# Feed-forward matmuls as pairs on the 128x64 halves of the array: a state-space convolution with a gated feed-forward

## The chip, the cores and the metric

The kernel runs on one core of one Trainium2 chip. Its time is the device time of one execution, in microseconds (us). The engines are named as the profile names them: PE is TensorE (PEld its weight loads), DVE VectorE, ACT ScalarE, POOL GpSimd, and SP the engine that issues most of the DMAs.

## What is computed

Everything is bfloat16, with one batch, 2048 positions and 512 channels. Cut to what matters:

```python
xn = layernorm(x)                                  # x = A_q, 2048 x 512
k_shift = sum(shift(k, t) * shift_k[:, t] for t in range(4))
kv = k_shift * v
y = irfft(rfft(kv, 4096) * rfft(ssm_k, 4096))[:2048] + kv * ssm_D
s = xn * y                                         # branch A: a long convolution
g = silu((gelu(xn @ w_gate) * (xn @ w_up)) @ w_down)   # branch B: 512 -> 1792 -> 512
out = x + s * g
```

The change concerns the three products of branch B: gate and up (512 to 1792) and down (1792 to 512).

## The kernel before

**Branch B** works in four quarters `q` of 512 positions, and in 14 units `m` of 128 hidden channels. `unit(q, m)` multiplies the 128 columns `m` of `Wg` and of `Wu` (four matmuls each, over the 512 inputs in blocks of 128) with the transposed quarter `xnT`, 512 positions wide, each product into a PSUM bank of its own. ScalarE takes the Gelu of the gate bank into `GE` (L1194), and VectorE multiplies it with the up bank into `HT` (L1203; for some units a copy `U_` of the up bank is multiplied instead, L1200). In the first quarter units 0 and 1 are cut to pieces of 128 positions (`N_HALF`), so that they can begin before the whole quarter is transposed. `down(q)` then sums, for each 128 positions of a quarter, 14 matmuls of `HT` with `Wd`, 512 columns wide, into one bank; the last 128 positions of the last quarter are cut into 384 and 128 columns.

**Branch A** is a transform of length 4096 in two stages. Its first stage uses the array as two halves of 64 rows (64x128 tiles; L959 for the filter, L950 for `kv`), its second stage and the first stage of the inverse use 16 tiles of 32x32 (L1028, in bursts of 16 or 32 matmuls), and the last stage of the inverse uses two halves of 64 columns (128x64 tiles, L1278). Between these stages the data go through DRAM (`ZH`, `ZK`, `ZI`). The filter `Hn` is first transposed on the whole array (L916).

**Three ways of using the array** matter here. A whole matmul (L641, by the helper `mm`) uses 128 rows and 128 columns. A pair on halves is two matmuls with `tile_position` (0, 0) and (0, 64): each has all 128 rows and 64 of the output rows (64 of the array's columns), both stream the same right-hand side, and together they fill the same 128 partitions of one bank. The downs of the last quarter were such pairs already (L1224), all but the last piece of 128 columns, since they lie among the pairs of L1278.

**Order.** The order of all engines' instructions is a list written out by hand (`SEQ`); `S.run()` walks it, gives out buffers (at most four single banks for branch B) and estimates times, from which the choice of buffers follows. A task's `mode` tells that estimate how the array is split. `trk.op` issues an instruction with the waits that its buffers need.

Of the kernel before, what the change touches and what calls it, by code (L numbers as in the profile page):

```python
# [17 lines left out]
KD = DM // 128  # L18
MF = FF // 128
NQ = 4  # L20
# [35 lines left out]
SMALL = 1.15 * 262144  # L56
T_FWD = 219.0
N_HALF = 2
UNITS = [(0, 6), (0, 8), (0, 10), (0, 12), (1, 0), (1, 2), (1, 4), (1, 6), (1, 8), (1, 10), (1, 12)]


# [352 lines left out]
def build_kernel(nc, A_q, A_k, A_v, A_shift_k, A_ssm_k, A_ssm_D, B_w_gate, B_w_up, B_w_down, out):  # L414
    with ExitStack() as es0:
# [18 lines left out]
        Wd = new("Wd", [128, MF, DM], BF16)  # L434
# [22 lines left out]
        xnT = new("xnT", [128, 2, 4, KD, 128], BF16)  # L457
# [6 lines left out]
        HT = new("HT", [128, 2, MF, 512], BF16)  # L464
# [51 lines left out]
        trk = Trk(nc, block)  # L516
# [9 lines left out]
        def bank(b):  # L526
            return PSALL[:, 512 * b.slot:512 * (b.slot + 1)]
# [4 lines left out]
        def R_bank(b):  # L532
            return [R_ps[b.slot // 2][b.slot % 2]]
# [106 lines left out]
        def mm(h, o, l, r, st, sp):  # L640
            return h.matmul(o, lhsT=l, rhs=r, start=st, stop=sp)  # L641


        B = Buf
        bX = [[B(f"X{q}_{t}") for t in range(4)] for q in range(NQ)]
# [137 lines left out]
        R_Wc = {}  # L783
# [381 lines left out]
        def unit(q, m):  # L1165
            ci = (m + 2) // 4
            pg, pu = B(f"psg{q}_{m}", pF), B(f"psu{q}_{m}", pF)
            g = B(f"ge{q}_{m}", pGE)

            def half(p, W, nm, j0=0, j1=4):  # L1170
                def f(e):
                    for kd in range(KD):
                        trk.op("PE", lambda h, kd=kd: mm(h, bank(p)[:, 128 * j0:128 * j1], W[:, kd, 128 * m:128 * (m + 1)], xnT[:, q % 2, j0:j1, kd, :], kd == 0, kd == KD - 1),
                               r=[R_Wc[nm, ci], *R_xnT[q % 2][j0:j1]], w=R_bank(p), accum=True)
                return f
            if q == 0 and m < N_HALF:

                for i in range(2):
                    c = slice(256 * i, 256 * i + 256)
                    p2 = [B(f"psg{q}_{m}_{i}", pF), B(f"psu{q}_{m}_{i}", pF)]  # L1180
                    g2 = B(f"ge{q}_{m}_{i}", pGE)
                    for p, W, nm in ((p2[0], Wg, "g"), (p2[1], Wu, "u")):
                        for j in (2 * i, 2 * i + 1):
                            gu_tasks[q].append(S.add([("PE", pe(4, 128))], half(p, W, nm, j, j + 1), r=[bW[nm][ci], bxnT[q][j]], w=[p], lat=150.0))
                    op([("ACT", act(256))], lambda e, h, p=p2[0], g=g2, c=c: h.activation(GE[:, g.slot, c], bank(p)[:, c], ACTF.Gelu_apprx_tanh), r=[p2[0]], w=[g2],
                       rr=lambda p=p2[0]: R_bank(p), ww=lambda g=g2: [R_GE[g.slot]], after=sin_tasks)
                    op([("DVE", dve(256, 1))], lambda e, h, p=p2[1], g=g2, c=c: h.tensor_tensor(HT[:, 0, m, c], bank(p)[:, c], GE[:, g.slot, c], ALU.mult), r=[p2[1], g2], w=[bHT[q][m]],
                       rr=lambda p=p2[1], g=g2: R_bank(p) + [R_GE[g.slot]], ww=[R_HT[0][m]])
                return
            tg = S.add([("PE", pe(4))], half(pg, Wg, "g"), r=[bW["g"][ci]] + bxnT[q], w=[pg], lat=150.0)  # L1190
            tu = S.add([("PE", pe(4))], half(pu, Wu, "u"), r=[bW["u"][ci]] + bxnT[q], w=[pu], lat=150.0, after=[tg])
            gu_tasks[q] += [tg, tu]
            af = sin_tasks if q == 0 else []
            op([("ACT", act(512))], lambda e, h: h.activation(GE[:, g.slot, :], bank(pg), ACTF.Gelu_apprx_tanh), r=[pg], w=[g],  # L1194
               rr=lambda: R_bank(pg), ww=lambda: [R_GE[g.slot]], after=af)
            af = (down_tasks[q - 2] if q >= 2 else []) + (s1_tasks["H"] if q == 1 else [])
            if (q, m) in UNITS:
                ub = B(f"ub{q}_{m}", pU)
                op(EV(512), lambda e, h: copy(e, h, U_[:, ub.slot, :], bank(pu)), r=[pu], w=[ub], rr=lambda: R_bank(pu), ww=lambda: [R_U[ub.slot]])
                op([("DVE", dve(512, 2))], lambda e, h: h.tensor_tensor(HT[:, q % 2, m, :], U_[:, ub.slot, :], GE[:, g.slot, :], ALU.mult), r=[ub, g], w=[bHT[q][m]],  # L1200
                   rr=lambda: [R_U[ub.slot], R_GE[g.slot]], ww=[R_HT[q % 2][m]], after=af)
                return
            op([("DVE", dve(512, 1))], lambda e, h: h.tensor_tensor(HT[:, q % 2, m, :], bank(pu), GE[:, g.slot, :], ALU.mult), r=[pu, g], w=[bHT[q][m]],  # L1203
               rr=lambda: R_bank(pu) + [R_GE[g.slot]], ww=[R_HT[q % 2][m]], after=af)

        def down(q):
            for jt in range(4):
                t = 4 * q + jt
                cols = [(0, DM)] if t < NT - 1 else [(0, 384), (384, DM)]
                for c0, c1 in cols:  # L1210
                    p = B(f"psd{q}_{jt}_{c0}", pF)

                    def pc(p=p, c0=c0, c1=c1):
                        return bank(p)[:, c0:c1]

                    for m0, m1 in ((0, 4), (4, 9), (9, 14)):
                        paired = q == NQ - 1 and c1 - c0 > 128

                        def f(e, p=p, jt=jt, m0=m0, m1=m1, pc=pc, c0=c0, c1=c1, paired=paired):
                            for m in range(m0, m1):  # L1220
                                if paired:
                                    for i in range(2):
                                        c = slice(64 * i, 64 * i + 64)
                                        trk.op("PE", lambda h, m=m, i=i, c=c: h.matmul(pc()[c, :], lhsT=HT[:, q % 2, m, 128 * jt + 64 * i:128 * jt + 64 * i + 64], rhs=Wd[:, m, c0:c1], start=m == 0, stop=m == MF - 1, tile_position=(0, 64 * i)),  # L1224
                                               r=[R_HT[q % 2][m], R_Wd[m // 7]], w=R_bank(p), accum=True)
                                    continue
                                trk.op("PE", lambda h, m=m: mm(h, pc(), HT[:, q % 2, m, 128 * jt:128 * (jt + 1)], Wd[:, m, c0:c1], m == 0, m == MF - 1),
                                       r=[R_HT[q % 2][m], R_Wd[m // 7]], w=R_bank(p), accum=True)
                        down_tasks[q].append(S.add([("PE", pe(m1 - m0, c1 - c0))], f, r=(bHT[q] if jt else bHT[q][m0:m1]) + bWd[m0 // 7:(m1 + 6) // 7],
                                                   w=[p], lat=150.0, mode=3 if paired else 0))  # L1230
                    n = c1 - c0
                    g, rg = G[:, t, c0:c1], [R_G[t] if n == DM else R_Gh[c0 > 0]]
                    bt = B(f"tanh{q}_{jt}")
                    if q < NQ - 1:
                        op([("ACT", act(n))], lambda e, h, g=g, pc=pc: h.activation(g, pc(), ACTF.Tanh, scale=0.5), r=[p], w=[bt],  # L1235
                           rr=lambda p=p: R_bank(p), ww=rg, after=h_tr_tasks + (h2_tasks if q >= 2 else []))
                        op([("DVE", dve(512, 1))], lambda e, h, g=g, pc=pc: h.scalar_tensor_tensor(out=g, in0=g, scalar=1.0, in1=pc(), op0=ALU.add, op1=ALU.mult),  # L1237
                           r=[p, bt], w=[bG[t // 2]], rr=lambda p=p, rg=rg: R_bank(p) + rg, ww=rg)
                        continue

                    u, x = XN[:, t, c0:c1], X[:, t, c0:c1]
                    b2 = B(f"o{t}_{c0}")
                    op([("ACT", act(n))], lambda e, h, g=g, pc=pc: h.activation(g, pc(), ACTF.Silu), r=[p], w=[bt],
                       rr=lambda p=p: R_bank(p), ww=rg, after=zh_tasks + h2_tasks)
                    op([("DVE", dve(n, 2))], lambda e, h, g=g, u=u: h.tensor_tensor(g, g, u, ALU.mult), r=[bt, bS[t // 2]], w=[b2], rr=rg + [R_XN[t]], ww=rg)
                    op([("DVE", dve(n, 2))], lambda e, h, g=g, x=x: h.tensor_tensor(g, g, x, ALU.add), r=[b2], w=[b2], rr=rg + [R_X[t]], ww=rg)
                    R_o, d_o = trk.free_res(f"outl{t}_{c0}"), dsem(f"d_outl{t}_{c0}")
                    d_out.append(d_o)
                    S.add([("SP", ISSUE)], lambda e, t=t, c0=c0, c1=c1, g=g, rg=rg, R_o=R_o, d_o=d_o: dma(e, out_dr[:, t, c0:c1], g, d_o, rg, [R_o]),
                          r=[b2], w=[B(f"outl{t}")], nbytes=256 * n)  # L1250
# [114 lines left out]
```

## Time and profile before

| | |
|---|---|
| median of 3 runs | 189.29 us (189.12 to 190.32) |
| the profiled execution | 189.28 us, of which 187.5 us are the span from its first to its last instruction |
| TensorE busy | 182.2 us, 1451 recorded matmuls, 1459 weight loads |
| VectorE, ScalarE, GpSimd busy | 164.8, 140.0, 12.9 us |
| DMA | 48.37 MB, mean 258 GB/s |

The page gives each engine's busy time as a share of the span. Matmuls overlap in the array, so the duration of one (about 0.38 us for 512 columns) is longer than its share of the stream; what one costs in a row of many is seen from the starts, or from the pieces of the chain of waits, which run from end to end.

### The profile page before, as it was taken

Reading aid. Unit: us, or ns where it says so; the run is one execution under the profiler, and the core shown is the slowest. Engines: PE = TensorE matmul, PEld = TensorE weight load, DVE = VectorE, ACT = ScalarE, POOL = GpSimd, SP = SyncE. Lnnn points to the kernel's source line nnn. Section 1 sums busy time; section 2 is a strip of 40 time slices with the busy share of each in tenths; the row PEclk is TensorE's granted clock in tenths of the full one; section 3 lists DMA queues with packets and bytes.
Section 4 is the critical chain, followed back from the end, with each engine's and each line's share of the span. In section 5 each row is a group of like instructions: output and inputs, shape, how many; then the busy total and the mean of one; then the engine's idle time right before and its main releaser. Section 6 shows DMA issues by size and latency. Waiting matters only on the chain.

```text
span 187.5 us, 3669 instructions
## 1 busy us (share of the span) xinstructions
PE 182.2 (97%) x1451; PEld 80.5 (43%) x1459; DVE 164.8 (88%) x249; ACT 140.0 (75%) x193; POOL 12.9 (7%) x26
## 2 busy tenths in 40 slices
PE   8899999999999999999999999999999999999993
PEld 3585443444334344334434433434333334445552
DVE  6897999999999999969459999998899994468995
ACT  3766697898698979888878779888887863144961
POOL 4502304100000000020200000000000000000000
PEclk9999999999999999999999999999999999999999
DMA  5999999999938695777999991869327056699226
GB/s 156 352 404 299 373 374 377 394 404 245 326 87 330 225 337 212 241 260 241 290 268 261 352 343 65 298 229 334 108 111 277 0 168 217 228 325 385 83 101 235
DMA packets 38502, 48.37 MB, mean 258 GB/s; under 512 B 9427, under 2 KB 28119, under 8 KB 38486
## 3 DMA queue, kind: packets, MB, share of 16 engines
q1 hardware_dynamic: 31958, 39.76, 64.1%
q10 hardware_dynamic: 6528, 8.39, 12.6%
q8 instruction: 11, 0.18, 0.5%
q14 instruction: 5, 0.04, 0.1%
HBM read 27.39 MB, written 14.68 MB: 224 GB/s over the span
## 4 chain that ended last, share of the span: by engine, by line
PE 91%; DVE 3%; DMA 2%; ACT 1%; issue 1%; POOL 0%
PE psall L641 71%; PE psall L1224 6%; PE psall L1028 6%; PE psall L950 2%; PE psall L959 2%; PE psall L916 2%; PE psall L1278 2%; DMA X<-in_A_q_dram 2%; ACT BO L632 1%; DVE stats L849 1%; DVE KAC L1005 1%; PE psall L892 0%; DVE XN L871 0%; DVE XN L965 0%; DVE HT L1203 0%
## 5 line engine op out<-in xcount | busy, mean ns | idle before, releaser
L641 PE MATMUL psall<-xnT,Wu 128*128 128x512 bf16 (+1 forms) x248 | 56.5, 359 | 0.0
L641 PE MATMUL psall<-xnT,Wg 128*128 128x512 bf16 (+1 forms) x248 | 55.8, 359 | 0.0
L1194 ACT ACTIVATE GE<-psall 128x512 bf16<-128x512 f32 x54 | 31.9, 606 | 13.6 <-PE psall L641 11.1
L641 PE MATMUL psall<-Wd,HT 128*128 128x512 bf16 (+1 forms) x174 | 38.3, 367 | 0.8 <-issue 0.6
L1203 DVE TENSOR_TENSOR HT<-psall,GE 128x512 bf16<-128x512 f32 x43 | 29.3, 682 | 7.8 <-PE psall L641 7.5
L641 PEld LDWEIGHTS psall<-xnT,Wu 128*128 128x128 bf16 x248 | 22.5, 98 | 26.1 <-issue 2.3
L641 PEld LDWEIGHTS psall<-xnT,Wg 128*128 128x128 bf16 x248 | 21.8, 98 | 26.0 <-issue 3.2
L632 ACT ACTIVATE BO<-psall 128x1024 bf16<-128x1024 f32 x20 | 19.9, 1022 | 9.4 <-PE psall L1278 4.8
L641 PEld LDWEIGHTS psall<-Wd,HT 128*128 128x128 bf16 x182 | 16.3, 98 | 21.2 <-issue 3.9
L1131 DVE TENSOR_TENSOR HSW<-KB,HSW 128x2048 bf16<-128x2048 bf16 x16 | 19.3, 1218 | 1.9 <-ACT KB L632 1.9
L632 ACT ACTIVATE HSW<-psall 128x1024 bf16<-128x1024 f32 x15 | 15.2, 1024 | 2.4 <-PE psall L1028 2.1
L632 ACT ACTIVATE KB<-psall 128x1024 bf16<-128x1024 f32 x15 | 14.6, 1026 | 0.8 <-PE psall L1028 0.8
L1011 DVE TENSOR_TENSOR KAC<-KAC,KTM 128x2048 bf16<-128x2048 bf16 x12 | 14.6, 1217 | 0.0
L1009 DVE TENSOR_TENSOR KTM<-KK,SKB 128x2048 bf16<-128x2048 bf16 x12 | 14.6, 1215 | 0.0
L632 ACT ACTIVATE AST<-psall 128x1024 bf16<-128x1024 f32 x12 | 12.1, 1032 | 0.9 <-PE psall L950 0.8
L1224 PE MATMUL psall<-Wd,HT 128*64 128x512 bf16 (+1 forms) x112 | 12.5, 366 | 0.0
L862 POOL TENSOR_TENSOR mv<-mv,NHALF 128x1 f32<-128x1 f32 (+1 forms) x7 | 7.3, 1049 | 68.6 <-DVE mv L850 48.0
L1235 ACT ACTIVATE G<-psall 128x512 bf16<-128x512 f32 x12 | 7.1, 597 | 6.3 <-PE psall L641 6.3
L849 DVE BATCH_NORM_STATS2 stats<-X 128x6 f32<-128x512 bf16 x16 | 10.5, 675 | 0.5 <-DMA X<-in_A_q_dram 0.5
L632 ACT ACTIVATE XN<-psall 128x1024 bf16<-128x1024 f32 x9 | 9.2, 1028 | 1.1 <-PE psall L959 1.0
L1237 DVE SCALAR_TENSOR_TENSOR G<-G,psall 128x512 bf16<-128x512 bf16 x12 | 7.9, 682 | 2.3 <-ACT G L1235 2.3
L1131 DVE TENSOR_TENSOR KB<-KB,HSW 128x2048 bf16<-128x2048 bf16 x8 | 9.7, 1219 | 0.1
(91 smaller groups left out, 178.3 us busy)
## 6 DMA issues: line engine op xcount, KB each, us to landing
BH<-ZH SPq DMA_DIRECT2D x8, 512.0 KB, 5.0
HSW<-HSW SPq DMA_DIRECT2D x16, 256.0 KB, 3.7
BK<-ZK SPq DMA_DIRECT2D x8, 512.0 KB, 5.9
ZI<-BO ACTq DMA_DIRECT2D x16, 256.0 KB, 2.8
BI<-ZI SPq DMA_DIRECT2D x8, 512.0 KB, 8.5
ZK<-AST SPq DMA_DIRECT2D x6, 512.0 KB, 2.9
ZH<-XN ACTq DMA_DIRECT2D x5, 512.0 KB, 4.3
Hn<-in_A_ssm_k_dram SPq DMA_DIRECT2D x4, 512.0 KB, 8.0
```

The costliest lines, as they stand in the source:

```text
L632: return h.activation(o, i, ACTF.Copy, scale=scale)
L641: return h.matmul(o, lhsT=l, rhs=r, start=st, stop=sp)
L849: t_stats[t] = op([("DVE", 670.0)], lambda e, h, t=t: h.bn_stats(stats[:, t, :], X[:, t, :]), r=[bX[q][t % 4]], w=[bst[t]], rr=[R_X[t]], w ...
L862: t_pw = op([("POOL", 2500.0 if q else 600.0)], lambda e, hd, ts=ts, n=n: hd.tensor_tensor(mv[:, ts, 3:4], mv[:, ts, 2:3], NHALF[:, 0:n, : ...
L1009: op([("DVE", dur)], lambda e, h, j=j, m=m: h.tensor_tensor(KTM[:, m.slot, :, :], kk(j), sk(j), ALU.mult), r=need + [bSKB[j], a], w=[m], r ...
L1011: op([("DVE", dur)], lambda e, h, m=m: h.tensor_tensor(KAC[:, a.slot, :, :], KAC[:, a.slot, :, :], KTM[:, m.slot, :, :], ALU.add), r=[m], ...
L1028: trk.op("PE", lambda h: h.matmul(ps(s, i)[b, :], lhsT=wt(col)[a, :], rhs=data(col)[a, :], start=n < 16, stop=n >= len(todo) - 16, tile_po ...
L1131: return hd.tensor_tensor(pair(KB, *(2 * DM * z for z in slots())) if to else x, k, x, ALU.mult)
L1194: op([("ACT", act(512))], lambda e, h: h.activation(GE[:, g.slot, :], bank(pg), ACTF.Gelu_apprx_tanh), r=[pg], w=[g], rr=lambda: R_bank(pg ...
L1203: op([("DVE", dve(512, 1))], lambda e, h: h.tensor_tensor(HT[:, q % 2, m, :], bank(pu), GE[:, g.slot, :], ALU.mult), r=[pu, g], w=[bHT[q][m]],
L1224: trk.op("PE", lambda h, m=m, i=i, c=c: h.matmul(pc()[c, :], lhsT=HT[:, q % 2, m, 128 * jt + 64 * i:128 * jt + 64 * i + 64], rhs=Wd[:, m, ...
L1237: op([("DVE", dve(512, 1))], lambda e, h, g=g, pc=pc: h.scalar_tensor_tensor(out=g, in0=g, scalar=1.0, in1=pc(), op0=ALU.add, op1=ALU.mult ...
```

## The change

Gate and up matmuls are issued as pairs on 128x64 halves in all units but 0 to 4 of the first quarter (`N_PLAIN`), and down matmuls as pairs in all quarters, except for the last piece of 128 columns. The left operand of each half is 64 of the 128 columns of the block, the right operand is the same for both. Whole matmuls stay for units 0 to 4 of the first quarter, the transposes, the warm-up and the last 128 columns. The order of the instructions on each engine and the modes that the estimate sees stay as they are: each whole matmul has two in its place.

```diff
+N_PLAIN = 5
...
+        def columns(o, l, r, st, sp, rr, ww):
+            for i in range(2):
+                c = slice(64 * i, 64 * i + 64)
+                trk.op("PE", lambda h, c=c, i=i: h.matmul(o[c, :], lhsT=l[:, c], rhs=r, start=st, stop=sp, tile_position=(0, 64 * i)), r=rr, w=ww, accum=True)
...
+            paired = q > 0 or m >= N_PLAIN
+
             def half(p, W, nm, j0=0, j1=4):
                 def f(e):
                     for kd in range(KD):
+                        if paired:
+                            columns(bank(p)[:, 128 * j0:128 * j1], W[:, kd, 128 * m:128 * (m + 1)], xnT[:, q % 2, j0:j1, kd, :], kd == 0, kd == KD - 1, [R_Wc[nm, ci], *R_xnT[q % 2][j0:j1]], R_bank(p))
+                            continue
...
-                        paired = q == NQ - 1 and c1 - c0 > 128
+                        paired = c1 - c0 > 128
...
+                                args = HT[:, q % 2, m, 128 * jt:128 * (jt + 1)], Wd[:, m, c0:c1], m == 0, m == MF - 1
+                                rw = [R_HT[q % 2][m], R_Wd[m // 7]], R_bank(p)
                                 if paired:
...
+                                    columns(pc(), *args, *rw)
+                                else:
+                                    trk.op("PE", lambda h, args=args: mm(h, pc(), *args), r=rw[0], w=rw[1], accum=True)
...
-                                                   w=[p], lat=150.0, mode=3 if paired else 0))
+                                                   w=[p], lat=150.0, mode=3 if paired and q == NQ - 1 else 0))
```

More of the change, by code (lines that the diff above doesn't have):

```diff
@@ L1216, in down @@
                     for m0, m1 in ((0, 4), (4, 9), (9, 14)):
-                        paired = q == NQ - 1 and c1 - c0 > 128
+                        paired = c1 - c0 > 128
                         def f(e, p=p, jt=jt, m0=m0, m1=m1, pc=pc, c0=c0, c1=c1, paired=paired):
                             for m in range(m0, m1):
+                                args = HT[:, q % 2, m, 128 * jt:128 * (jt + 1)], Wd[:, m, c0:c1], m == 0, m == MF - 1
+                                rw = [R_HT[q % 2][m], R_Wd[m // 7]], R_bank(p)
                                 if paired:
[L1222 to L1228, printed above, removed]
+                                    columns(pc(), *args, *rw)
+                                else:
+                                    trk.op("PE", lambda h, args=args: mm(h, pc(), *args), r=rw[0], w=rw[1], accum=True)
                         down_tasks[q].append(S.add([("PE", pe(m1 - m0, c1 - c0))], f, r=(bHT[q] if jt else bHT[q][m0:m1]) + bWd[m0 // 7:(m1 + 6) // 7],
-                                                   w=[p], lat=150.0, mode=3 if paired else 0))
+                                                   w=[p], lat=150.0, mode=3 if paired and q == NQ - 1 else 0))
                     n = c1 - c0
```

## The prediction

> **What bounds the kernel now.** First the page: the engines' shares, the granted clock, and the chain that ended last.
>
> ```profile
> PE 182.2 (97%) x1451; PEld 80.5 (43%) x1459; DVE 164.8 (88%) x249; ACT 140.0 (75%) x193; POOL 12.9 (7%) x26
> ...
> PEclk9999999999999999999999999999999999999999
> ...
> PE 91%; DVE 3%; DMA 2%; ACT 1%; issue 1%; POOL 0%
> ```
>
> TensorE is busy 97% of the span, it holds 91% of the chain, and its clock is full in all forty slices. Next, what TensorE waited for, in the list of waits filtered to it, and under it a row of the view of the tile `psall` with the whole-array down products:
>
> ```profile
> PE psall L641 <- PEq L1350: 0.8, 1, 0.8
> PE psall L641 <- issue: 0.6, 4, 0.2
> PE psall L892 <- DVE XN L871: 0.5, 1, 0.5
> PE psall L959 <- DVE HT L1203: 0.3, 1, 0.3
> ...
> L641 PE MATMUL psall<-Wd,HT x174: 219/379/390, 39.0 to 184.4; 128*128 128x512 bf16 x160, 128*128 128x128 bf16 x14
> ```
>
> These are four waits, 2.2 us in all. From about 24 us on nothing but TensorE's own stream sets the end, so the change is worth what it does to that stream. (The "issue" gaps I read as missing matmul records: the down products have 174 where the program has 168 + 14 = 182.)
>
> The chain in order of time gives that stream in pieces, each timed from the end of the piece before it to its own end: start, duration, line and number of matmuls. The last row, from the groups by line and form, is the pairs' weight loads (busy us, mean ns of one).
>
> ```profile
> 63.49 4.42 PE psall L641 x20
> ...
> 76.45 1.83 PE psall L641 x8
> ...
> 100.64 4.42 PE psall L641 x20
> 105.06 0.37 PE psall L1028 x16
> 105.43 2.69 PE psall L641 x12
> 108.12 0.58 PE psall L1028 x32
> 108.70 1.83 PE psall L641 x8
> ...
> 168.79 0.55 PE psall L1278 x4
> 169.35 1.94 PE psall L1224 x18
> ...
> 174.09 0.43 PE psall L1278 x4
> ...
> L1224 PEld LDWEIGHTS psall<-Wd,HT 128*64 128x64 bf16 x112 | 6.3, 110 | 5.2
> ```
>
> L641 pieces are whole-array matmuls, L1028 the bursts on 32x32 tiles, L1224 and L1278 the pairs on 128x64 halves that exist already. Twelve more whole matmuls (20 against 8) cost 4.42 - 1.83 = 2.59 us, so one costs 0.216. What is left of a piece, 1.83 - 8 x 0.216 = 0.10 us, is the price of entering whole-array mode, and it is the same behind 32x32 tiles (100.64, 108.70) and behind the 64x128 matmuls of L950 (63.49, 76.45).
>
> **The change: the stream itself.** 432 whole gate and up matmuls of 512 columns exist (12 undivided units of four for gate and four for up in the first quarter, 14 in each other quarter). Units 2, 3 and 4 of the first quarter keep 24 of them, so 408 become pairs, and with them the 3 x 4 x 14 = 168 down matmuls of the first three quarters. 576 matmuls become 576 pairs, 1152 matmuls of half the output rows with the same 512 columns streamed. A pair's price is in the trace: 18 matmuls of L1224, nine pairs, took 1.94 us, 0.216 a pair. That is the whole matmul's price to the last digit. Steady streaming therefore changes by 576 x 0 = 0. What hides the doubled weight loads is that they run under the matmul before: a load of a half takes 0.110 us and both of a pair run side by side (6.3 us busy for 112), beneath 0.216 of streaming. If that cover failed, 576 x 0.11 = 63 us would stand open; the 1.94 shows no part of it.
>
> [...]
>
> **The change: entering and leaving.** In the order of the changed kernel's TensorE instructions a stretch of pairs is entered 36 times at a place where a stretch of whole matmuls was entered before: 24 times from 32x32 tiles, 12 times from 64x128 matmuls. Each has an exit as before. Beside them, two switches are new early (a later unit's gate and up come there as pairs, the Hn transposes and the last of units 2 to 4 behind them whole), one is new where a transpose of Hn is followed by pairs at about 25 us, and the one at 168.7 us, where whole matmuls gave way to L1278, goes.
>
> What entering pair mode costs, the trace shows once, at 168.79: 0.55 us for two pairs that otherwise take 0.43 (174.09), so 0.12, against 0.10 for whole matmuls. The tile view shows the difference more finely (shortest, median and longest ns of one):
>
> ```profile
> L641 PE MATMUL psall<-xnT,Wg x248: 219/379/390, 7.5 to 166.7; 128*128 128x512 bf16 x108, 128*128 128x128 bf16 x16
> ...
> L1278 PE MATMUL psall<-BI,G x32: 379/379/403, 168.7 to 180.6; 128*64 128x512 bf16 x32
> ```
>
> The first matmul after a switch waits for its weights: 390 - 379 = 11 ns on the whole array, 403 - 379 = 24 on halves. I take 13 ns for each of the 36 entries: 36 x 0.013 = 0.47 us.
>
> [...]
>
> The switch itself, without the weights, in the timeline (each window opened so that the last matmul or pair before a switch stands alone):
>
> ```profile
> 118.69 0.38 PE L641 MATMUL psall<-xnT,Wu 128*128 128x512 bf16 x1
> 119.00 0.43 PE L1028 MATMUL psall<-BH,TF 32*32 32x512 bf16 x16
> 119.37 0.39 PE L641 MATMUL psall<-xnT,Wg 128*128 128x512 bf16 x1
> ...
> 168.41 0.38 PE L641 MATMUL psall<-xnT,Wu 128*128 128x512 bf16 x1
> 168.72 0.62 PE L1278 MATMUL psall<-BI,G 128*64 128x512 bf16 x4
> ...
> 183.38 0.33 PE L1224 MATMUL psall<-Wd,HT 128*64 128x384 bf16 x2
> 183.64 0.95 PE L641 MATMUL psall<-Wd,HT 128*128 128x128 bf16 x14
> ```
>
> From whole to tiles 0.31 us start to start, from whole to pairs 0.31, against 0.216 without a switch: 0.095 each. From pairs of 384 columns to whole 0.26, where 384 columns stream in 0.75 x 0.216 = 0.16: 0.10. So all kinds cost alike, whether the columns alone are re-split or both rows and columns. The 72 switches that matter (pairs to and from tiles, pairs to and from 64x128) are not in the trace. Their change is bounded below by a drain that vanishes, -0.1 each or -7 us; above, by a switch that waits until the modelled end of a matmul, 0.38 instead of 0.31 us, +0.07 each or +5. I take zero, since four kinds lie within 10 ns.
>
> The odd switches: the one that goes saves 0.12 at 168.7, the one at 25 us costs 0.12, in sum nothing. The two early ones cost 0.12 + 0.10 = 0.22 us, ahead of this wait:
>
> ```profile
> 22.02 1.21 DVE L1005 TENSOR_TENSOR KAC<-KK,SKB 128x2048 bf16<-128x2048 bf16 x1
> 23.16 0.67 DVE L1203 TENSOR_TENSOR HT<-psall,GE 128x512 bf16<-128x512 f32 x1
> ...
> 20.05 1.03 PE L641 MATMUL psall<-xnT,Wu 128*128 128x512 bf16 x4
> ...
> 23.88 0.39 PE L959 MATMUL psall<-HTr,F 64*128 64x512 bf16 x2 [0.31 <-DVE HT L1203]
> ```
>
> TensorE stands idle 0.31 us there, for an HT product that VectorE does late because KAC runs first; its up input, by the order the group that starts at 20.05, had ended at 21.08, 2 us earlier. 0.22 fits under 0.31; without that cover it is +0.22.
>
> No DMA, wait or buffer moves: the order on every engine is the same, and consumers of a pair wait for its second half. ScalarE and VectorE keep their instructions.
>
> The sum against the profiled run, 189.28 us (187.5 of span and 1.8 around it; the median is 189.29): 0 + 0.47 + 0 = 189.75, say 189.8.
>
> **The rivals.** *Cheaper switches (faster).* If a change between two column-split modes drains less than one to or from the whole array, each of the 72 gains up to 0.1 us: half of it gives 189.8 - 3.6 = 186.2, all of it 182.6. It decides beyond 1% from (1.9 + 0.5) / 72 = 33 ns a switch. For it: none of these 72 is in the trace. Against it: whole to pairs re-splits columns alone and still pays 0.095.
>
> *Instruction issue (slower).* A pair needs four instructions where a whole matmul needs two. The tightest long stretch:
>
> ```profile
> 109.00:155.60 46.60, 46.31 (x541) 18.31 (x542) 45.04 (x49) 38.77 (x50) 0.00 (x0) 1.00 0.56 191
> ...
> 7.63 1.16 PE psall L641 x20
> ```
>
> 1083 instructions in 46.6 us, 43 ns each. The bursts in it are 9 of 16 and 7 of 32 tiles, 368 matmuls; the other 173 double, so 1429 must be issued, 33 ns each. Small early matmuls were fed at 1.16 / 40 = 29 ns an instruction, but over 20 matmuls only, which a queue may have held ready. If the sustained rate lies over 33 ns, TensorE starves around the bursts: at 36 ns the stretch takes 51.4 us, +4.8, so 194.6; it passes 1% from about 34. Against it: the 1.94 of L1224 is 54 ns an instruction without strain, and matmul time alone explains the 43.
>
> **How the numbers follow.** A measurement of this kernel can't tell under about 1% (1.9 us) from no change. The forecast gets 0.72; its own spread is the early 0.22 and some ns a switch, 189.0 to 190.8. Cheaper switches get 0.18, of which 0.13 beyond 1%; issue gets 0.10, of which 0.09 beyond. So faster 0.13, same 0.72 + 0.05 + 0.01 = 0.78, slower 0.09. The range leaves out the large outcomes of both rivals: 187.4 (33 ns a switch gained) to 191.2 (1% up, or 20 ns lost a switch).
>
> **What would show it.** Right: pieces of pairs in the chain at 0.216 a pair plus 0.12 where whole ones had 0.10; bursts still 0.36 to 0.37 and 0.58; TensorE gaps as before. Wrong: the first start behind a burst of 16 other than 0.37 us after the burst's own (119.00 to 119.37), an exit from pairs unlike 0.31, or new TensorE gaps put down to issue between 109 and 156 us.

## The result and the profile after

The changed kernel takes 190.16 us (median of 22 runs, beside 189.47 for 22 runs of the kernel before): a ratio of 1.0044, 95% interval 1.0031 to 1.0056, so 0.83 us more (0.59 to 1.06). The ratio is worked out from all of these runs; the two medians alone lie 0.69 us apart. The profiled execution took 190.05 us with a span of 188.2.

The page's clock and the other engines' shares stand as before, and TensorE holds 96% of the chain that ended last, where it held 91%. What grew is TensorE's count of instructions:

```profile
PE 184.2 (98%) x2035; PEld 89.6 (48%) x2035; DVE 165.2 (88%) x249; ACT 140.4 (75%) x193; POOL 12.9 (7%) x26
...
PEclk9999999999999999999999999999999999999999
...
q8 instruction: 16, 0.26, 0.5%
...
PE 96%; DVE 2%; ACT 1%; issue 0%
```

The row `q8 instruction` is from the list of DMA queues: the number of packets and the MB in which TensorE's own program is fetched, and the share of the 16 DMA engines' time that they took. Before, the same row was

```profile
q8 instruction: 11, 0.18, 0.5%
```

That this row is TensorE's is read from its growth: the only other such row, `q14 instruction`, has 5 packets and 0.04 MB in both, and the other engines' counts stand.

The chain in order of time (start, duration, line, matmuls), the same places as before; L647 are the pairs, so 24 and 16 matmuls stand where 12 and 8 stood, and the burst lines are now L956 and L1034:

```profile
76.90 1.85 PE psall L647 x16
...
101.21 4.44 PE psall L647 x40
...
106.01 2.71 PE psall L647 x24
108.72 0.58 PE psall L1034 x32
109.31 1.85 PE psall L647 x16
...
169.64 0.43 PE psall L1287 x4
170.07 1.94 PE psall L647 x18
```

Each piece is 0.02 longer, whatever its length: 1.83 became 1.85 and 4.42 became 4.44. So twelve pairs more still cost 4.44 - 1.85 = 2.59 us, 0.216 each, and the bursts still 0.58. The 0.55 of the inverse's first two pairs at 168.79 is 0.43, as everything around it is now in pairs.

The same in the starts of two bursts far apart, from the timelines of before (L1028) and after (L1034):

```profile
81.45 0.43 PE L1028 MATMUL psall<-BH,TF 32*32 32x512 bf16 x16
...
154.87 0.65 PE L1028 MATMUL psall<-HSW,MI 32*32 32x512 bf16 x32
```
```profile
81.93 0.43 PE L1034 MATMUL psall<-BH,TF 32*32 32x512 bf16 x16
...
155.70 0.65 PE L1034 MATMUL psall<-HSW,MI 32*32 32x512 bf16 x32
```

The second kernel is 0.48 us late at the first and 0.83 at the second. Between them lie 23 stretches of branch B: 0.35 / 23 = 0.015 us a stretch.

The tile view (shortest, median, longest ns) and the switches in the timeline (the last two matmuls in front of a burst, the burst, the first pair behind it):

```profile
L647 PE MATMUL psall<-xnT,Wg x408: 379/379/403, 19.3 to 167.5; 128*64 128x512 bf16 x136
```
```profile
118.70 1.03 PE L647 MATMUL psall<-xnT,Wu 128*64 128x512 bf16 x8
119.66 0.43 PE L1034 MATMUL psall<-BH,TF 32*32 32x512 bf16 x16
120.03 0.62 PE L647 MATMUL psall<-xnT,Wg 128*64 128x512 bf16 x4
```

First pairs take 403 ns, as forecast. From burst to pairs it is 0.37 us (119.66 to 120.03), as it was from burst to whole. TensorE's list of waits is shorter than before:

```profile
PE psall L642 <- PEq L1359: 0.8, 1, 0.8
PE psall L898 <- DVE XN L877: 0.2, 1, 0.2
```

One wait isn't in it, since matmuls overlap (379 ns long, one every 216): near 50.9 us the second of two groups on the 64x128 halves starts late. In the chain that piece has 0.69, where the same piece usually has 0.54:

```profile
47.86 0.54 PE psall L965 x4
48.40 2.28 PE psall L647 x20
50.68 0.69 PE psall L965 x4
```

It waits for a bank that ScalarE copies into `X`, and that copy began at 48.84 us instead of 47.96, with no work ahead of it on ScalarE. `X` there holds an earlier group until its store to DRAM has landed. The view of DMAs has that store (KB, us from issue to landing), issued at 43.35 us before:

```profile
ZH<-X ACTq DMA_DIRECT2D x1, 512.0 KB, 4.2
```

and at 43.65 us after:

```profile
ZH<-X ACTq DMA_DIRECT2D x1, 512.0 KB, 5.1
```

It landed at 48.76 us, and the copy began 0.08 us later. So the copy was late because the store was.

### The profile page after: what moved, and what is told of

Read it like the earlier page. It is cut to its first block, busy times and chain, and to the rows that moved or that the text cites. A ratio compares the mean times of both kernels' runs of the same rounds, so it can differ in the third digit from the quotient of the medians.

```text
span 188.2 us, 4829 instructions
## 1 busy us (share of the span) xinstructions
PE 184.2 (98%) x2035; PEld 89.6 (48%) x2035; DVE 165.2 (88%) x249; ACT 140.4 (75%) x193; POOL 12.9 (7%) x26
## 4 chain that ended last, share of the span: by engine, by line
PE 96%; DVE 2%; ACT 1%; issue 0%
PE psall L647 75%; PE psall L642 7%; PE psall L1034 6%; PE psall L965 2%; PE psall L956 2%; PE psall L922 2%; PE psall L1287 2%; DVE KAC L1011 1%; PE psall L898 0%; DVE XN L971 0%; DVE HT L1214 0%; ACT xnT L633 0%; DVE G L1255 0%; DVE G L1254 0%; ACT G L1252 0%
## 5 line engine op out<-in xcount | busy, mean ns | idle before, releaser
L647 PE MATMUL psall<-Wd,HT 128*64 128x512 bf16 (+1 forms) x448 | 51.5, 377 | 0.0
L647 PE MATMUL psall<-xnT,Wu 128*64 128x512 bf16 x408 | 50.9, 380 | 0.0
L647 PE MATMUL psall<-xnT,Wg 128*64 128x512 bf16 x408 | 50.5, 381 | 0.0
L647 PEld LDWEIGHTS psall<-Wd,HT 128*64 128x64 bf16 x448 | 24.4, 110 | 24.0 <-issue 3.7
L647 PEld LDWEIGHTS psall<-xnT,Wu 128*64 128x64 bf16 x408 | 22.4, 110 | 21.9 <-issue 1.6
L647 PEld LDWEIGHTS psall<-xnT,Wg 128*64 128x64 bf16 x408 | 21.5, 110 | 22.4 <-issue 3.0
L633 ACT ACTIVATE KB<-psall 128x1024 bf16<-128x1024 f32 x15 | 14.6, 1024 | 1.4 <-PE psall L1034 1.4
L1160 DVE TENSOR_TENSOR HSW<-HSW 128x2048 bf16<-128x2048 bf16 x8 | 9.6, 1216 | 0.0
```

The source lines that it names most:

```text
L633: return h.activation(o, i, ACTF.Copy, scale=scale)
L647: trk.op("PE", lambda h, c=c, i=i: h.matmul(o[c, :], lhsT=l[:, c], rhs=r, start=st, stop=sp, tile_position=(0, 64 * i)), r=rr, w=ww, accum ...
L1160: return hd.tensor_tensor(x, x, y, ALU.add)
```

## The experiments

Theory W is that of the prediction, with the measured 0.0145 us a stretch: 36 x 0.0145 = 0.52 us (the first expectations still reckon with 11 ns, so 0.40). Its rivals changed as runs came in. Ratios are to the kernel before on the same chip, with 95% intervals.

| run | ratio | interval |
|---|---|---|
| changed kernel again | 1.0044 | 1.0026 to 1.0062 |
| pairs in the last stretch only | 0.9995 | 0.9974 to 1.0016 |
| late start of pairs | 1.0072 | 1.0045 to 1.0098 |
| quarters instead of halves | 1.0095 | 1.0069 to 1.0120 |
| kernel before, 78 instructions longer | 1.0074 | 1.0046 to 1.0102 |
| late start, 78 instructions longer | 1.0065 | 1.0043 to 1.0087 |
| changed kernel, 78 instructions longer | 1.0030 | 1.0007 to 1.0052 |
| late start, 24 instructions shorter | 1.0011 | 0.9988 to 1.0033 |
| kernel before, 26 instructions longer | 0.9980 | 0.9958 to 1.0003 |
| whole and pairs alternating | one run of 199.08 us | |

**The changed kernel again.** No edit.

> The changed kernel unaltered, to see which differences of its trace come again. Theory W (what is paid is the wait for the first weights of each stretch of pairs, net 11 ns at 36 entries, 0.40 us, and one switch that the cover of the early part doesn't hide): slower than before by 0.5 to 0.9 us; the first matmul behind a 32x32 burst again has 403 ns and the next starts 240 ns later. Rival J (part of it is chance): the 0.14 us wait of the transforms' second group near 50.9 us and VectorE's 0.13 us delay near 18 us are gone or elsewhere. Rival S (each pair streams some 1.2 ns longer than a whole matmul, 576 x 1.2 = 0.7 us): pieces of 40 pair matmuls in the chain take over 4.45 us in every repeat.

The ratio came again to the last digit. The first pairs again have 403 ns. Pieces of 40 are 4.44, not over 4.45, but S's own sum for them is 4.42 + 20 x 0.0012 = 4.444, so they don't decide. The starts do: near 55 us, from the second to the twentieth matmul of a piece before, and from the second to the twentieth pair after, it is 3.885 us alike, where S would have 0.02 more. The wait near 50.9 us came again, a little shorter (0.64 in place of 0.69); VectorE's 0.13 us did not.

**Pairs in the last stretch only.** Edit (`cnt["tiles"]` counts the 32x32 bursts issued so far; there are 24), the same condition in `down`:

```diff
-                        if paired:
+                        if paired and cnt["tiles"] == 24:
```

> Pairs only in the last long stretch, behind the last 32x32 burst, where the following pairs make the switch at 168.7 us unnecessary; all else whole, as before. Theory W: 35 of the 36 entries go, one remains (+0.011 us), the switch goes (-0.12 us): 0.11 us under before, 189.3 to 189.4 where before is 189.47; in the chain no 0.55 for the first pairs of the inverse's last stage but 0.43. Rival S: 61 pairs x 1.2 ns = +0.07, so 0.05 under before. The two are told apart by the length of the stretch: 13.27 + 0.01 us (W) or 13.34 (S).

In the chain of this run:

```profile
155.56 0.58 PE psall L1038 x32
156.14 13.29 PE psall L649 x122
169.43 0.43 PE psall L1291 x4
```

and in that of the kernel before:

```profile
154.94 0.58 PE psall L1028 x32
...
168.79 0.55 PE psall L1278 x4
```

61 pairs take 13.29 us; the 61 whole ones took 168.79 - (154.94 + 0.58) = 13.27. That is W's +0.01 or 0.02, not S's +0.07, and S falls. Between the last burst and the inverse's first pair this kernel gained 0.08 us on the kernel before, by the starts in the two traces. The time, 0.9995, can't show so little.

**A late start of pairs.** Edit (`cnt["first"]` counts the transforms' first-stage groups of the filter):

```diff
-                        if paired:
+                        if paired and cnt["first"] >= 8:
```

> As the changed kernel, but whole matmuls until the 64x128 burst at about 30 us, so that the three new switches of the early part (two near 20 us, one at 25 us) are gone; entries from bursts as in the changed kernel. Theory W: the switch at 25 us costs 0.12, the two near 20 us lie under the wait for VectorE: 0.12 us faster than the changed kernel, about 0.5 to 0.6 above before. If the early cover had failed: 0.25 to 0.34 faster than the changed kernel. Rival S: 24 pairs fewer of 576, so 0.03 faster than the changed kernel plus the switches.

A miss: 1.0072 is 1.4 us above before, and the forecast 0.5 to 0.6 lies under its interval. (Slower than the changed kernel isn't shown, the two intervals overlap.) TensorE was hardly late. Its last matmul started at 184.61 us, 0.23 behind the kernel before. What was late is the end of the run: the span ended 3.04 us after VectorE's last product, where it ends 2.04 after it in the kernels before and after. The view of DMAs in the last microseconds (median us from issue to landing at the end of each row), before:

```profile
out_dram<-G SPq DMA_DIRECT2D x1, 96.0 KB, 1.6
out_dram<-G SPq DMA_DIRECT2D x1, 32.0 KB, 1.5
```

and with the late start:

```profile
q8 instruction: 1, 0.02, 0.6%
...
out_dram<-G SPq DMA_DIRECT2D x1, 96.0 KB, 2.6
out_dram<-G SPq DMA_DIRECT2D x1, 32.0 KB, 2.3
```

In that window a packet of TensorE's program was fetched, at 184.1 us, 16 KB that took 0.93 us. The kernel before had its last fetch at 174.4, the changed one at 180.6. Fetches come about every 250 recorded instructions, weight loads counted (249 in the changed kernel, 251 with quarters). This gave theory F, at that point a supposition: a fetch holds one of the 16 DMA engines, and a transfer that passes then lands later.

The packets fit it. As the fetch ends, at 185.07 us, packets of the output stores begin to follow one another in single file, each starting as the one before it ends, and after 187.16 us, when all other packets are through, this file alone goes on for 0.63 us. What the DMA engines moved in slices of 0.05 us shows it, before (from 185.0 us) and with the late start (from 186.2, as far from the end of the run):

```profile
GB/s 246 123 144 307 369 348 369 328 328 205 205 21 0 0 0 0 0 0 154 261 338 307 338 292 185 93 0 5 138 210 190 88 26 0 0 0 0 0 0 0
```
```profile
GB/s 287 369 185 123 144 241 261 394 307 348 241 108 87 41 56 210 200 154 92 26 20 20 20 20 31 15 31 15 31 10 20 10 0 0 0 0 0 0 0 0
```

Before, the last store ends at once. With the late start a tail of 10 to 31 GB/s is left, and one file with 1024 B every 42 ns, as its packets come there, is 24. The other two traces that end late have the same tail, 0.8 us long; the nine that end 2.04 or 2.05 us after the last product have none.

**Quarters.** Edit, up to the last burst; behind it halves:

```diff
-            for i in range(2):
-                c = slice(64 * i, 64 * i + 64)
+            n = 64 if cnt["tiles"] == 24 else 32
+            for i in range(128 // n):
+                c = slice(n * i, n * i + n)
```

> As the changed kernel, but up to the last 32x32 burst every pair is four matmuls on quarters of 32 columns (128x32), eight instructions where a whole matmul has two. Theory W, with a weight load whose exposed time goes with the columns of a tile (64: 24 ns; 32x32 tiles show 10 to 11): the first matmul behind a burst has 390 ns and the next set starts 226 to 229 ns later, 0.4 us less than the changed kernel, 0.3 to 0.4 us above before; sets stream at 216 ns. Rival S (cost per extra matmul): 1.4 us above before or more. Rival I (issue: TensorE gets an instruction every 29 ns or slower): eight instructions in 216 ns are 27 ns each, and between 109 and 156 us 2 x (368 + 4 x 173) = 2120 in 46.6 us are 22 ns each, so the stretch takes 2120 x 0.029 = 61 us or longer, 15 us above before.

In the tile view and the chain of this run (sets of four matmuls, so x48 is twelve):

```profile
L650 PE MATMUL psall<-xnT,Wg x792: 379/379/390, 19.4 to 167.6; 128*32 128x512 bf16 x192, 128*64 128x512 bf16 x6
```
```profile
116.79 0.36 PE psall L1039 x16
117.16 2.70 PE psall L650 x48
119.86 0.36 PE psall L1039 x16
```

First sets have 390 ns, as on the whole array, the second set starts 226 or 227 ns behind the first, and twelve sets take 2.70 where twelve whole ones took 2.69. On the two column tiles tried, what a first matmul lasts above 379 ns goes with the columns, as W said: 24 ns for 64, 11 for 32. The whole array's 128 columns don't fit that row, they have 11 too. The issue rival falls: 1036 matmuls and as many loads in this stretch, 22 ns an instruction, without a gap of TensorE in it:

```profile
111.20:156.10 44.90, 44.87 (x1036) 19.60 (x1036) 42.92 (x47) 37.28 (x47) 0.00 (x0) 1.00 0.58 192
```

Yet the time, 1.0095, isn't W's 0.3 to 0.4 us but 1.8. The profiled run was the fastest of this kernel, 190.06 us, 0.78 above the kernel before's, and 0.45 us of that is one wait at 110.8 us in front of a burst that reads a transfer; what is left, 0.33, is what W forecast. The other runs that the ratio counts took 190.7 to 191.6 us. Where they lost the rest, no trace of them shows. Its program took 24 fetches.

**78 instructions more.** The warm-up, whose results are used nowhere, in pieces of 128 columns: the same columns, 39 matmuls and 39 loads more. It was put on the kernel before, the late start and the changed kernel:

```diff
-            for i in range(N_WARM):
-                trk.op("PE", lambda h: mm(h, bank(warm), ONE[:, 0:128], ONE, True, True), w=R_bank(warm), accum=True)
+            for i in range(4 * N_WARM):
+                trk.op("PE", lambda h: mm(h, bank(warm)[:, 0:128], ONE[:, 0:128], ONE[:, 0:128], True, True), w=R_bank(warm), accum=True)
```

> The kernel before, with its 13 warm-up matmuls of 512 columns as 52 of 128 (the same columns in sum; warm-up results are used nowhere): 78 more TensorE instructions at the start, nothing else. Theory F (TensorE's program comes in fetches of 16 KB, one about every 256 instructions; each holds one of the 16 DMA engines for about 1 us, and a transfer that the end waits for lands later by up to that): before has its eleventh and last fetch at 174.4 us; with 78 instructions more a twelfth falls some 20 instructions before the end, near 184 us, into the last output transfers: span and time about 1.0 us longer than before, with TensorE's own end unmoved to 0.1 us. Rival C (the late end of the run with the late start was chance): the same time as before to 0.2 us.

The kernel before became 0.74% slower, 1.4 us. TensorE's last matmul started 0.14 us earlier than before, but the run ended 3.21 us after VectorE's last product. In its last microseconds:

```profile
q8 instruction: 1, 0.02, 1.1%
...
out_dram<-G SPq DMA_DIRECT2D x1, 96.0 KB, 2.8
out_dram<-G SPq DMA_DIRECT2D x1, 32.0 KB, 2.5
```

The twelfth fetch came, at 182.0 us and not near 184 as forecast.

> The kernel with the late start of pairs, with the same 52 warm-up matmuls. Theory F: its last fetch, at 184.1 us without them, moves to near 180 us, and the last output transfer again lands 2.0 us after the last VectorE product instead of 3.0: 0.7 to 1.0 us faster than without them, so 0.4 to 0.5 above before, and 0.1 under the changed kernel. Rival C: the same time as without them, 190.7.

Half a miss. The fetch moved to 181.0 us and the run ended 2.05 us after the last product, as F said, but another fetch now lay at 45.8. The store from `X` took 6.4 us to land (4.6 without the longer program), and TensorE waited for ScalarE's copy into `X`, at the place where the changed kernel had its small delay:

```profile
PE psall L968 <- ACT X L633: 1.2, 2, 0.7
```

So the time stayed where it was.

> The changed kernel with the same 52 warm-up matmuls. Its fetches all move some 78 instructions ahead, the one at 45.6 us to near 41. Theory F: ScalarE's copy into X near 48.8 us, which came 0.6 us late in both profiles of the changed kernel, comes about 48.2, and TensorE's wait of 0.11 to 0.14 us at 50.9 is gone; what is left above before is 36 stretches x 0.0145 = 0.52, plus 0.12 for the switch at 25 us, less 0.10 for the one at 168.7: 0.5 us. Rival C: the wait comes and goes without regard to the fetches; no difference to the changed kernel in the median.

Here the fetch at 45.6 us moved to 40.7. The store from `X` landed in 3.9 us instead of 5.1, and the second group's delay was gone (0.54 for the piece, as elsewhere):

```profile
48.14 0.54 PE psall L965 x4
48.68 2.28 PE psall L647 x20
50.95 0.54 PE psall L965 x4
```

The ratio, 1.0030, is 0.57 us, where 0.5 was forecast. Its interval overlaps that of the changed kernel, so that in the time alone the 0.14 us isn't shown.

**Two tests that F could fail.** The late start moved on by one burst (`>= 9`), 24 instructions shorter, so that the last fetch should fall away; and the kernel before with its warm-up in 26 pieces of 256 columns, 26 instructions longer, too few for a twelfth fetch.

> As the kernel with the late start of pairs, but pairs begin one 64x128 burst later, at 33 us: 12 pairs fewer, so 24 TensorE instructions fewer. Theory F: the fetch that fell at 184.1 us, some 18 instructions before the end, isn't needed before the program ends, so the last output transfer lands 2.0 us after the last VectorE product, not 3.0, and the time is 1.0 us under that of the late start; with theory W (35 stretches x 0.0145 = 0.51, less 0.10 for the switch at 168.7) 0.4 us above before. Rival C (the fetches don't matter): 0.01 us under the late start, 1.2 to 1.4 above before.

> The kernel before with its 13 warm-up matmuls of 512 columns as 26 of 256: 26 TensorE instructions more instead of the 78 of the longer program. Theory F: a twelfth fetch would be due some 24 instructions later than the program has them at the end, so there is none, the last transfer lands 2.0 us after the last product, and the time is that of before to 0.2 us. Rival X (a warm-up cut to smaller matmuls is itself what made the longer program slow): up to 1 us above before here too.

Both went as F said. The shorter late start ended 2.04 us after the last product, with its last fetch at 173.7, at a ratio of 1.0011 where the longer one had 1.0072; W's 0.4 us (1.0022) lies in its interval. The kernel before with 26 instructions more had eleven fetches and a time like before (0.9980), so that cutting up the warm-up cost nothing by itself.

**Whole and pairs alternating.** In the long stretch behind the last burst every second matmul is whole (`kd` or `m` even).

> The changed kernel, but in the long stretch behind the last 32x32 burst every second matmul is whole again, so that whole matmuls and pairs alternate: 30 whole and 31 pairs, about 59 switches more. Theory W (a switch between whole and pairs costs its drain, 0.095 us, and the first weights, 0.011 for whole and 0.024 for pairs): 29 x 0.107 + 30 x 0.120 = 6.7 us more, the stretch takes 20.0 us instead of 13.3, the time is about 196.8. Rival D (drains between single matmuls overlap, or a switch between modes that differ in columns alone is cheaper when short): under 4 us more.

```profile
158.46 0.32 PE psall L642
158.79 0.34 PE psall L649 x2
159.12 0.32 PE psall L642
159.44 0.34 PE psall L649 x2
```

A whole matmul and a pair take 0.66 us end to end instead of 2 x 0.216, so 0.114 a switch. From the last burst's start to the inverse's first pair this trace has 6.70 us more than the changed kernel's, as W forecast; switches that follow at every matmul don't overlap here, at 0.114 each, and rival D falls. The run as a whole was 2.3 us above the forecast: its two groups near 50 us came 1.1 us late, with a fetch at 47.1 and 6.0 us to the landing of the store from `X`, and it ended 2.97 us after the last product, with a fetch at 191.7.

## Why the prediction was right

The forecast was 189.8 us, 0.47 above the kernel before's run; measured were 0.83 (0.59 to 1.06). That is inside the range and the likeliest case, but 0.47 lies under the interval. The mechanism held, and its term came out at 0.52; the rest came from places that the prediction put at nothing, and that they were small is in part luck. Its premise that under 1% can't be told from no change was too cautious: 22 runs of each told 0.44%.

- *Steady streaming costs nothing.* Right: 0.216 us a pair in every piece, 61 pairs in 13.29 us against 13.27.
- *36 entries at 13 ns.* Right in mechanism, a little small. Starts in the traces give it apart: the second pair of a stretch starts 240 ns after the first, where the second whole matmul started 226 or 227 after, so +13.5; the first start behind a burst comes 2 to 3 ns sooner; and the second half of each pair starts 3 ns behind the first, which the exit then counts from, +3. That makes about 0.0145 us, and 0.52 in place of 0.47. The weight loads themselves differ by as much: one lasts 98 ns for the whole array, 110 for a half, 97 for a quarter.
- *72 switches of kinds not in the trace cost what the others do.* Right: from the last matmul's start to the burst's 309 ns as before, to 64x128 311 or 312, back 304 to 306 or 314 to 317. The cheaper switches that the rival bet on are 2 to 3 ns cheaper, not 33. (The 59 switches of the alternating run are between whole matmuls and pairs, a kind that the trace of before had.)
- *The odd switches.* Right. At 25 us the new one costs 0.12 and at 168.7 the old one's 0.12 is gone. The two near 20 us stayed under the wait for VectorE, but only just: they put TensorE 0.32 us behind, not 0.22, as the transposes behind the second take 0.55 us instead of 0.44, and the wait was 0.31. TensorE's group behind it started at 24.01 instead of 23.88, but VectorE was 0.13 us behind already at 18.6, before the first new switch.
- *Issue.* Wrong as a rival, rightly at a low chance: 22 ns an instruction went through without a gap.
- *"No DMA, wait or buffer moves."* This step failed, though little hung on it. The kernel issues the same DMAs, but TensorE's program grew from 11 fetches to 16, which the page counts among the DMA packets, at other times. In the changed kernel one of them, at 45.6 us, goes with a store that lands late, a late copy and 0.14 us of waiting; moved to 40.7, the wait is gone.

The sum with what the runs showed, in the profiled run: 0.52 for the stretches, 0.12 - 0.12 for the odd switches, 0.14 for the wait near 50.9 us, 0.13 for VectorE's delay at 18.6, and -0.07 that the prediction didn't have either, in all 0.72, beside 0.73 between the two spans. The -0.07 lies near 54 us: from one 64x128 burst to the next it is 5.25 us in all four traces with whole matmuls there, and 5.18 to 5.20 in all eight with pairs or quarters, one entry included. Why is not shown. VectorE's 0.13 us is chance: the repeat reached the burst at 30 us at the same time as the kernel before, 0.25 us sooner than the first trace, and its span is 0.42 longer than before. Over the twelve traces that burst starts anywhere from 29.5 to 30.8 us, whichever kernel it is.

How far the traces carry F: by the pages TensorE's 2910 recorded matmuls and weight loads took 11 packets before, 4070 took 16 in the changed kernel and 6130 took 24 with quarters, which is 265, 254 and 255 for each packet of 16 KB. With the late start the last two output transfers landed 2.6 and 2.3 us after their issue, where before it was 1.6 and 1.5: 0.8 to 1.0 us later, behind a packet of 0.93 us. That the late packets come in single file from the end of the fetch on fits F's reading that both went through one engine, but the trace doesn't number the engines, so it is not shown. For the wait near 50.9 us the landing of the store from `X` tells. In the four traces with a fetch at 45.3 to 47.1 us, while the store is on its way, it took 5.1, 5.1, 6.0 and 6.4 us to land, and each time the copy began 0.08 us after the landing; with a fetch at 47.3, shortly before the landing, 4.6; in the seven without one, 3.7 to 4.8. So a store can be slow without a fetch, but the two runs that moved a fetch out of this place or into it moved the wait with it. Still open is where the quarters lose 1.4 us in a usual run.

## What to carry to other kernels

In this kernel splitting matmuls over column halves neither cost nor gained in a steady stream of 512 columns (0.216 us for a pair as for a whole matmul); it cost 0.0145 us for each stretch between bursts of another mode, and gained a whole switch (0.1 us) where the neighbours were pairs already. So pair what borders on pairs, and nothing else: here that is the last stretch alone, where the starts show 0.08 us gained and the time is too coarse to show it. And the instruction count had a cost beside its issue, 1.4 us for 78 more at the start of the kernel before: look where the program's fetches fall, above all in the last microseconds and beside transfers that something waits for.

## What the runs showed of the hardware

In the three traces with a 16 KB fetch of TensorE's program in the last 4.6 to 6.5 us, the run ended 0.9 to 1.2 us later than usual (2.97 to 3.21 us after VectorE's last product instead of 2.04 or 2.05); in five others with the last fetch more than 7.3 us before the end it ended as usual. 78 harmless instructions at the start of the kernel before were enough to bring a late end about. The first matmul of a stretch lasted 403 ns on halves of 64 columns, 390 on quarters of 32 and 390 on the whole array of 128, where those behind it lasted 379; the difference, 24, 11 and 11 ns, is read as the wait for its weights, since at 120.03 us in the changed kernel the loads of the first pair start with it, and those of the next pair 0.21 us ahead of theirs.
